# Padding the gate-decay matmuls to 128 rows and splitting the second FFN product by its high and low parts

## The chip, the cores and the metric

The kernel runs on one core of a Trainium2 chip. The metric is the device time of one execution in microseconds (us). The engines are named as in the profile: PE (matrix products; PEld is its weight loads), DVE (vector), ACT (scalar), POOL (GpSimd) and SP (queue that issues most DMAs). SBUF is the on-chip memory, PSUM holds the products of PE.

## What is computed

An mLSTM layer with exponential gates, over 4 batches, 8 heads, 768 steps and heads of width 40, followed by a gated feed-forward layer (FFN) of width 1024:

```python
m_new = np.maximum(f_gate[:, :, t] + m, i_gate[:, :, t])
f_stab = np.exp(f_gate[:, :, t] + m - m_new)
i_stab = np.exp(i_gate[:, :, t] - m_new)
C = f_stab[..., None, None] * C + i_stab[..., None, None] * np.einsum('bhd,bhe->bhde', vt, kt)
n = f_stab[..., None] * n + i_stab[..., None] * kt
h_tilde = np.einsum('bhde,bhe->bhd', C, qt)
denom = np.maximum(np.abs(np.einsum('bhd,bhd->bh', n, qt)), 1.0)[..., None]
y[:, :, t] = sigmoid(o_gate[:, :, t]) * h_tilde / denom
...
h = np.maximum(x @ w_in, 0.0)                    # x: the heads side by side, width 320
conv_out[:, t] = sum(conv_w[k] * h[:, t + k - 1] for k in range(3))
out = (h * sigmoid(conv_out)) @ w_out
```

## The kernel before

**Tiling.** The 768 steps of a batch are cut into 6 chunks of 128, so there are 24 chunks s; two chunks make one of 12 units u of 256 steps for the FFN. Within a chunk attention is a matrix product with decays; between chunks a state `Cst` (40 x 41 per head, three heads side by side in a group, so 120 rows) carries over.

**Gates.** `gates` (L242 to L258) runs two scans and two sums over 32 rows (batch x head) on DVE for a group of chunks. `GS` cuts the 6 chunks into groups (0,1), (1,2), (2,6), so the last group is four chunks wide. `gates_t` transposes the results on PE and `gates_tc` copies them out: `aT` on DVE (L306), `wT` on ACT (L308).

**Decays.** For the first three chunks (`NP` = 3) the decays are spread by PE: `ch_gpe` (L401) adds a triangular mask (one matmul of 512 columns, L405) and then, per head, a product of one column of the identity, repeated 128 times, with the 32 rows of `Gt` (L408). For all later chunks a DMA spreads them from DRAM and POOL masks them (L432). ACT takes the exponential (`ch_exp`, L439).

**Attention of a chunk.** `ch_s` (L464) forms scores in PSUM, `ch_p` (L471, DVE) multiplies by the decays, `ch_inter` (L482) multiplies the queries with the masked state `cb`, `ch_pv` (L491) adds the products with the values into the same PSUM tile `pY`, of which there is one. `ch_rden` makes the denominator, `ch_num` (L547, DVE) divides out of `pY` into `x`, `ch_x` (L554, DVE) applies the output gate on `x` in SBUF, `ch_t` (L575) transposes it, `ch_split` and `ch_splitl` (L213, L589, L590) cut it into a high and a low part. `ch_u` and `ch_state` (L502, L515) advance the state, `ch_cb` (L518) multiplies it with a mask of 120 x 369 numbers, `mk_sb`: two instructions, all on POOL.

**Weights.** `w_in` and `w_out` come as 64-bit numbers, 17 loads with the convolution's weights; each is converted by one ACT, four DVE (or POOL) instructions (`w_abs` L326, `w_max` L330, `w_conv` L339, L341, L343) and cut into a high and a low part.

**FFN of a unit.** Eight blocks f of 128 columns. `f_m1` (L618) is eight matmuls; `f_relu`, `f_tap1`, `f_tap` (L628, L636, L650) make the convolution, then for each pair of blocks `f_tanh`, `f_g` (L654, L658), `f_gh` (the high part, ACT, L213) and `f_gl` (the low part, POOL, L209). `f_m2` (L672) multiplies for each block f and each half k of the unit three times (L681): high part by high weights, high part by low weights, low part by high weights, into two PSUM tiles `po`. `f_out` (L683) evicts both halves on one engine and `f_outd` stores them.

**Order.** Every step is a job with costs by engine, a priority (`z` plus an offset by kind, `OFF`), an earliest time (`REL`, `SLOPE`) and the jobs that it follows. `order` (L85) is a list scheduler that runs when the program is built: it fixes the order in which each engine gets its instructions; on the chip each engine runs its own list in that order and waits by semaphores. It also puts in products of zeros (`warm`, L358, one call is two instructions) where it plans a gap of PE, after 16 such calls at the start.

Of the kernel before, what the change touches and what calls it, by code (L numbers as in the profile page):

```python
# [28 lines left out]
GS = ((0, 1), (1, 2), (2, 6))  # L29
OFF = dict(  # L30
    gpe=-466.23, loadw=661.3, mask=-269.35, loadn=-68.02, o=280.76, exp=294.49, wk=-126.2, u=148.37, state=-639.08,
    cb=374.33, s0=-143.64, s1=77.22, p0=75.42, p1=778.82, inter=-156.65, pv0=139.58, pv1=72.13, rd0=-530.16,
    rd1=-177.78, rd2=-366.75, num=-71.97, x=-364.12, dup=-443.23, t=134.98, split=-103.1, splitl=-629.56, halo=-96.74,
    xnew=770.29, kz=422.26, eg=-465.52, qe=-64.53, m1=68.78, relu=280.55, tap1=-76.28, tap0=-31.97, tap2=-344.77,
    tanh=-878.29, g=-168.6, gh=-221.34, gl=-54.96, m2=172.63, out=-699.14, outd=-271.95, wld=-396.31, wabs=113.45,
    wc0=142.39, wc1=134.61, wc2=-231.53, wc3=-361.52, wsh=-403.2, wsl=-141.82, g0=139.41, ga0=-702.7, gw0=202.06,
    ge0=-294.32, gd0=185.74, gg0=-506.27, ta0=-379.4, tc0=84.31, tw0=-397.4, tx0=499.3, g1=-646.44, ga1=106.16,
    gw1=-15.09, ge1=-15.86, gd1=135.02, gg1=240.52, ta1=81.59, tc1=-75.67, tw1=-9.9, tx1=-551.62, g2=489.66,
    ga2=-137.32, gw2=-158.94, ge2=92.62, gd2=-67.67, gg2=-504.91, ta2=-274.22, tc2=-450.62, tw2=-181.8, tx2=-88.05,
# [27 lines left out]
FREE0 = dict(PE=6.15, DVE=3.5, ACT=5.8, POOL=5.2, SP=1.6)
# [18 lines left out]
def order(jobs, pre):  # L86
# [31 lines left out]
    while len(done) < len(jobs):  # L118
# [42 lines left out]
        else:  # L161
            d = j["cost"][e]
            if e == "PE":
# [10 lines left out]
                for a, b, w in spans:  # L174
                    while a < b:
# [3 lines left out]
                        if c <= a:  # L179
                            break  # L180
# [693 lines left out]
```

## Time and profile before

| what | value |
|---|---|
| median of 3 runs | 345.4 us (345.09 to 349.81) |
| the profiled execution | 344.72 us |
| its span, first to last instruction | 342.6 us |
| mean granted clock of PE | 0.959 |
| PE, DVE, ACT, POOL busy | 328.7, 262.9, 236.3, 202.7 us |

Times in the rows below are from the span's start. A "busy" PE is one with a matmul in flight, which at the lower of its two clock levels says little about work done, so the granted clock of a stretch is read beside it. The idle time that stands in a row is that of the engine just before the instruction, with the engine and the tile that ended it.

### The profile page before, as it was taken

How to read it: one execution, taken by the hardware profiler on the slowest of the kernel's cores; microseconds unless marked ns; L12 is line 12 of the kernel's file. 1: busy time of each engine (PE TensorE's matmuls, PEld its weight loads, DVE VectorE, ACT ScalarE, POOL GpSimd, SP SyncE). 2: the span in 40 equal slices, each digit the busy share in tenths (PEclk: the TensorE clock that was granted, in tenths of full speed). 3: DMA queues.
4: the chain of work that ended last, by engine and by line, in shares of the span. 5: the costliest groups of instructions: out<-in, count | busy, mean ns of one | idle time of the engine just before them, and what ended most of it. 6: DMA issues, size and time to landing. Idle time of an engine off the chain costs nothing.

```text
span 342.6 us, 7422 instructions
## 1 busy us (share of the span) xinstructions
PE 328.7 (96%) x2534; PEld 322.3 (94%) x2534; DVE 262.9 (77%) x598; ACT 236.3 (69%) x610; POOL 202.7 (59%) x310
## 2 busy tenths in 40 slices
PE   7699898998999999999999999999999999999995
PEld 7588898999999999999999999999999999999995
DVE  4897889999998987778489877676888768566750
ACT  2355747879988668896958786769685536577871
POOL 7369898869968647584745661746563234343341
PEclk9855599999999999999999999999999999999999
DMA  6887658686717466174315452654211001010111
GB/s 167 273 250 299 215 196 271 192 256 180 221 53 219 150 194 205 64 216 157 101 58 153 127 160 93 187 182 147 94 59 41 0 2 38 2 38 2 38 41 38
DMA packets 18575, 46.09 MB, mean 135 GB/s; under 512 B 2579, under 2 KB 6347, under 8 KB 18539
## 3 DMA queue, kind: packets, MB, share of 16 engines
q1 hardware_dynamic: 18068, 45.22, 42.4%
q8 instruction: 20, 0.33, 0.5%
q10 hardware_dynamic: 471, 0.41, 0.4%
q14 instruction: 16, 0.13, 0.1%
HBM read 41.49 MB, written 4.13 MB: 133 GB/s over the span
## 4 chain that ended last, share of the span: by engine, by line
PE 71%; DVE 11%; POOL 6%; ACT 4%; DMA 3%; issue 3%; SPq 0%; POOLq 0%; DVEq 0%; ACTq 0%
PE po L681 22%; PE ph L618 22%; PE pY L491 10%; PE pS L464 9%; PE pY L482 3%; PE pU L502 3%; PE pT L575 2%; DMA wraw<-in_w_in 1%; DVE cv L650 1%; DVE ph L650 1%; ACT w L439 1%; DMA w<-G_d 1%; PE pg L408 1%; POOL gl L209 1%; POOL w L432 1%
## 5 line engine op out<-in xcount | busy, mean ns | idle before, releaser
L209 POOL TENSOR_TENSOR gl<-cv,gh 128x512 fp32r<-128x512 f32 x48 | 62.5, 1302 | 47.4 <-ACT gh L213 40.7
L618 PE MATMUL ph<-X,wi_h 128*128 128x258 f32 x480 | 77.1, 290 | 2.2 <-DVE cv L650 1.5
L618 PEld LDWEIGHTS ph<-X,wi_h 128*128 128x128 f32 x480 | 64.6, 190 | 3.0 <-ACT ph L636 1.7
L681 PE MATMUL po<-wo_h,gh 128*128 128x320 f32 x192 | 61.5, 320 | 0.5 <-ACT ot L687 0.5
L439 ACT ACTIVATE w<-w,aT 128x128 f32<-128x128 f32 x168 | 55.1, 391 | 8.1 <-POOL w L432 8.1
L650 DVE SCALAR_TENSOR_TENSOR ph<-h,cw_sb,ph 128x256 f32<-128x256 f32 x96 | 46.1, 483 | 18.9 <-ACT ph L636 18.4
L681 PE MATMUL po<-wo_l,gh 128*128 128x320 f32 x192 | 59.3, 309 | 0.0
L681 PE MATMUL po<-wo_h,gl 128*128 128x320 f32 x192 | 59.3, 309 | 0.0
L464 PE MATMUL pS<-q,kz 120*128 120x128 f32 (+1 forms) x384 | 53.1, 287 | 4.2 <-DVE aT L306 3.1
L464 PEld LDWEIGHTS pS<-q,kz 120*128 120x128 f32 (+1 forms) x384 | 48.6, 199 | 4.6 <-DVE aT L306 3.2
L658 DVE SCALAR_TENSOR_TENSOR cv<-cv,h 128x512 f32<-128x512 f32 x48 | 40.4, 844 | 15.9 <-ACT cv L654 15.6
L628 ACT ACTIVATE h<-ph 128x258 f32<-128x258 f32 x96 | 36.5, 380 | 23.1 <-PE ph L618 21.2
L650 DVE SCALAR_TENSOR_TENSOR cv<-h,cw_sb,ph 128x256 f32<-128x256 f32 x96 | 45.1, 476 | 8.1 <-POOL gl L209 4.9
L618 PE MATMUL ph<-X,wi_l 128*128 128x258 f32 x288 | 50.3, 283 | 0.0
L491 PE MATMUL pY<-n,w 128*128 128x41 f32 x384 | 47.8, 282 | 0.0
L491 PEld LDWEIGHTS pY<-n,w 128*128 128x128 f32 x384 | 47.2, 197 | 0.2
L636 ACT ACTIVATE ph<-h,cw_sb 128x256 f32<-128x256 f32 x96 | 45.6, 475 | 1.9
L654 ACT ACTIVATE cv<-cv 128x512 f32<-128x512 f32 x48 | 30.1, 627 | 16.3 <-DVE cv L650 9.3
L618 PEld LDWEIGHTS ph<-X,wi_l 128*128 128x128 f32 x288 | 41.3, 190 | 0.0
L213 ACT ACTIVATE gh<-cv 128x512 fp32r<-128x512 f32 x48 | 30.0, 624 | 11.2 <-PE po L681 11.2
L681 PEld LDWEIGHTS po<-wo_h,gh 128*128 128x128 f32 x192 | 36.2, 188 | 0.7 <-ACT ot L687 0.7
L681 PEld LDWEIGHTS po<-wo_l,gh 128*128 128x128 f32 x192 | 36.2, 189 | 0.0
(84 smaller groups left out, 530.0 us busy)
## 6 DMA issues: line engine op xcount, KB each, us to landing
n<-in_nat SPq DMA_DIRECT2D x24, 484.0 KB
w<-G_d SPq DMA_DIRECT2D x21, 512.0 KB
q<-in_qT SPq DMA_DIRECT2D x12, 360.0 KB
out<-ot SPq DMA_DIRECT2D x24, 160.0 KB
wraw<-in_w_in SPq DMA_DIRECT2D x8, 384.0 KB
kz<-in_kT SPq DMA_DIRECT2D x24, 120.0 KB
eq<-E_d SPq DMA_DIRECT2D x24, 120.0 KB
wraw<-in_w_out SPq DMA_DIRECT2D x8, 320.0 KB
```

What stands on the lines that cost most here:

```text
L209: (nc.gpsimd if e == "POOL" else nc.vector).tensor_tensor(out=out, in0=in0, in1=in1, op=op)
L213: nc.scalar.activation(out, in_, AF.Copy)
L439: nc.scalar.activation(w[:, h, :], g, AF.Exp, bias=aT[:, c, b * 8 + h : b * 8 + h + 1])
L464: nc.tensor.matmul(pS[:, j, :], lhsT=lhsT, rhs=rhs, start=(j == 0), stop=(j == 3), skip_group_check=True)
L491: nc.tensor.matmul(pY[:, h * VW : (h + 1) * VW], lhsT=r["w"][:, n, :], rhs=v[:, DM + h * VW : DM + (h + 1) * VW], start=(c == 0 and n == 0 ...
L618: nc.tensor.matmul(ph, lhsT=a, rhs=b_, start=(i == 0), stop=(i == len(mm) - 1))
L628: nc.scalar.activation(hj, ph, AF.Relu)
L636: nc.scalar.activation(c, hk, AF.Copy, scale=wk)
L650: nc.vector.scalar_tensor_tensor(o, hk, wk, c, op0=ALU.mult, op1=ALU.add)
L654: nc.scalar.activation(cv, cv, AF.Tanh, scale=0.5)
L658: nc.vector.scalar_tensor_tensor(cv, cv, 1.0, h[:, :, 1 : 1 + UT], op0=ALU.add, op1=ALU.mult)
L681: nc.tensor.matmul(obuf[u][k], lhsT=a, rhs=b_, start=(f == 0 and i == 0), stop=(f == 7 and i == 2))
```

## The change

1. `Gt` becomes the first 32 rows of a tile `Gz` of 128 rows; the other 96 rows are set to zero by two DVE instructions. The spread of the decays multiplies all 128 rows.
2. `GS` has four groups: (0,1), (1,2), (2,4), (4,6).
3. The mask is 120 x 3 numbers, and `ch_cb` is three ACT instructions with a scale per row, in place of two POOL ones. POOL clears `Cst` once at the start.
4. `ch_num` divides in place in PSUM; `ch_x` reads PSUM and writes `x`. So `pY` is held until `x` is done, and not only until `num` is.
5. `m2` becomes two jobs for each block: `m2` (high part, two matmuls for each half) that waits for `gh`, and `m2l` (low part, one for each half) that waits for `gl` and `m2`. `gl` must now be done before `gh`'s buffer is used again.
6. `out` and `outd` become one job for each half.
7. The starting calls of `warm` go from 16 to 9, the planner's constants and offsets are new, and a table `FIX` gives the jobs of the first six chunks, of all weights, of the first two units and of the end priorities and earliest times of their own.

```diff
-GS = ((0, 1), (1, 2), (2, 6))
+GS = ((0, 1), (1, 2), (2, 4), (4, 6))
...
-    Gt = const.tile([32, S], F32, name="Gt")
+    Gz = const.tile([P, S], F32, name="Gz")
+    nc.vector.memset(Gz[32:64, :], 0.0)
+    nc.vector.memset(Gz[64:P, :], 0.0)
+    Gt = Gz[0:32, :]
...
-            nc.tensor.matmul(p[:, j, :], lhsT=id_sb[0:32, r : r + 1].to_broadcast([32, P]), rhs=Gt[:, c * P : (c + 1) * P],
+            nc.tensor.matmul(p[:, j, :], lhsT=id_sb[:, r : r + 1].to_broadcast([P, P]), rhs=Gz[:, c * P : (c + 1) * P],
...
+    nc.gpsimd.memset(Cst, 0.0)
...
-    def ch_cb(e, s):
+    def ch_cb(s):
         cb = sb.tile([120, 3, 123], F32, name="cb", tag="cb")
-        mk3 = mk_sb.rearrange("p (g v) -> p g v", g=3)
-        tt(e, cb[:, 0:2, :], Cst[:, 0:2, :], mk3[:, 0:2, :], ALU.mult)
-        tt(e, cb[0:80, 2, 0:82], Cst[0:80, 2, 0:82], mk3[0:80, 2, 0:82], ALU.mult)
+        for j in range(3):
+            ng, sl = 3 if j < 2 else 2, slice(j * VW, (j + 1) * VW)
+            nc.scalar.activation(cb[:, 0:ng, sl], Cst[:, 0:ng, sl], AF.Copy, scale=mk_sb[:, j : j + 1])
...
     def ch_num(s):
...
-        nc.vector.tensor_tensor(x, y3[:, :, 0:D], r["rd"].unsqueeze(2).to_broadcast([P, H, D]), op=ALU.mult)
-        r["x"] = xf
+        nc.vector.tensor_tensor(y3, y3, r["rd"].unsqueeze(2).to_broadcast([P, H, D]), op=ALU.mult)
 
     def ch_x(s):
...
-        nc.vector.scalar_tensor_tensor(xf[:, 0:DM], o, 1.0, xf[:, 0:DM], op0=ALU.add, op1=ALU.mult)
+        nc.vector.scalar_tensor_tensor(x, o, 1.0, y3, op0=ALU.add, op1=ALU.mult)
...
-    def f_m2(u, f):
+    def f_m2(u, f, low):
...
+        ws = [wo_h[:, f, :]] if low else [wo_h[:, f, :], wo_l[:, f, :]]
         for k in range(2):
-            mm = ((gh[:, j, ks], wo_h[:, f, :]), (gh[:, j, ks], wo_l[:, f, :]), (gl[:, j, ks], wo_h[:, f, :]))
+            for i, w in enumerate(ws):
+                nc.tensor.matmul(obuf[u][k], lhsT=g[:, j, k * P : (k + 1) * P], rhs=w, start=(f == 0 and not low and i == 0), stop=(f == 7 and low == 1))
...
-        at("inter", z, qe + [("cb", us - 1)] if c else [], ch_inter, s, ring="y", users=[("num", s), ("rd1", s)], cost=0.63 if c else 0.01)
+        at("inter", z, qe + [("cb", us - 1)] if c else [], ch_inter, s, ring="y", users=[("x", s)], cost=0.63 if c else 0.01)
...
-            at("m2", n, [("gl", 4 * u + f // 2), ("wsl", 8 + f)] + ...
+            at("m2", n, [("gh", 4 * u + f // 2), ("wsl", 8 + f)] + ...
+            at("m2l", n, [("gl", 4 * u + f // 2), ("m2", n)] + ([("m2l", n - 1)] if n else []), f_m2, u, f, 1)
+        for k in range(2):
+            at(f"out{k}", 8 * u, [("m2", 8 * u + 7), ("m2l", 8 * u + 7)], f_out, u, k, ring="ot", users=[(f"outd{k}", u)])
+            at(f"outd{k}", 8 * u, [(f"out{k}", u)], f_outd, u, k)
```

## Rows read from the trace of the kernel before

**Rows 1.** Busy time and granted clock by stretch: us, busy us of each engine (instructions), PEclk, DMA.

```profile
14.10:41.40 27.30, 24.79 (x103) 21.60 (x104) 24.30 (x46) 17.14 (x53) 21.23 (x34) 0.50 0.78 263
41.40:60.00 18.60, 17.09 (x150) 16.57 (x150) 16.27 (x41) 11.09 (x34) 17.45 (x28) 1.00 0.74 233
60.00:140.00 80.00, 78.11 (x651) 77.10 (x650) 73.13 (x178) 65.75 (x186) 59.72 (x94) 1.00 0.60 179
140.00:300.00 160.00, 160.00 (x1300) 159.92 (x1299) 118.94 (x276) 111.87 (x274) 82.20 (x132) 1.00 0.32 101
```

**Rows 2.** PE in order of time, front: start, length in us, work, idle before.

```profile
1.81 6.45 PE L358 MATMUL pw<-wz 128*128 128x128 f32 x32 [1.81 <-POOL wz L352]
8.02 0.48 PE L405 MATMUL pg<-tri 128*128 128x512 f32 x1
...
15.52 2.08 PE L464 MATMUL pS<-q,kz 120*128 120x128 f32 x8 [3.07 <-DVE aT L306]
...
20.98 2.07 PE L408 MATMUL pg<-Gt,id_sb 32*128 32x128 f32 x8
...
23.89 3.64 PE L491 MATMUL pY<-n,w 128*128 128x41 f32 x16
...
37.63 2.05 PE L464 MATMUL pS<-q,kz 120*128 120x128 f32 x8 [1.09 <-DVE X L590]
...
41.81 1.99 PE L464 MATMUL pS<-q,kz 120*128 120x128 f32 x16
```

**Rows 3.** ACT in order of time, the start, as in rows 2.

```profile
6.74 0.31 ACT L228 ACTIVATE tri<-ltm 128x128 fp32r<-128x128 f32 x1 [2.34 <-DMA ltm<-in_tr]
```

**Rows 4.** Waits in the first 50 us: us in total, times, longest us.

```profile
DVE rd L534 <- PE pY L491: 2.3, 1, 2.3
...
DVE w L471 <- PE pS L464: 1.4, 2, 1.2
```

**Rows 5.** DVE in order of time, 9 to 16 us, as in rows 2.

```profile
10.22 0.36 DVE L330 TENSOR_SCALAR wmag<-wmag 128x384 f32<-128x384 f32 x1 [1.40 <-ACT wmag L326]
10.49 1.27 DVE L246 TENSOR_TENSOR_SCAN mt<-ft,mt,it 32x512 f32<-32x512 f32 x1
...
12.51 1.63 DVE L254 TENSOR_TENSOR Gt<-Gt,mt 32x512 f32<-32x512 f32 x1
...
15.31 0.15 DVE L306 COPY aT<-pt 128x32 f32<-128x32 f32 x1
15.55 2.15 DVE L330 TENSOR_SCALAR wmag<-wmag 128x384 f32<-128x384 f32 x1
```

**Rows 6.** Groups by line: instructions, busy us, mean ns of one, idle before.

```profile
L209 POOL TENSOR_TENSOR cb<-Cst,mk_sb 120x246 f32<-120x246 f32 (+1 forms) x40 | 22.3, 577 | 5.5 <-DVE Cst L513 5.0 <-DVE Cst L515 0.5
...
L554 DVE SCALAR_TENSOR_TENSOR x<-n,x 128x320 f32<-128x320 f32 x24 | 14.7, 612 | 0.3
...
L343 DVE SCALAR_TENSOR_TENSOR wf<-wraw,wf 128x384 int32<-128x384 int32 (+1 forms) x16 | 12.5, 787 | 0.1
...
L547 DVE TENSOR_TENSOR x<-pY,rd 128x320 f32<-128x320 f32 x24 | 11.7, 486 | 0.5
...
L213 ACT ACTIVATE x<-x 128x64 f32<-128x64 f32 x15 | 3.7, 250 | 5.9 <-DVE x L554 5.9
```

**Rows 7.** The instructions of L554: least, median and most ns, first and last start.

```profile
L554 DVE SCALAR_TENSOR_TENSOR x<-n,x x24: 479/491/1429, 30.3 to 295.1; 128x320 f32<-128x320 f32 x24
```

**Rows 8.** PE waits from 60 us on, as in rows 3.

```profile
PE ph L618 <- DVE cv L650: 1.5, 3, 0.9
PE ph L618 <- ACT wo_h L213: 0.6, 1, 0.6
PE po L681 <- ACT ot L687: 0.5, 1, 0.5
```

**Rows 9.** The end in order of time, as in rows 2.

```profile
338.52 0.88 ACT L687 ACTIVATE ot<-po 128x320 f32<-128x320 f32 x2 [4.36 <-PE po L681]
...
338.98 0.81 SPq L697 DMA_DIRECT2D out<-ot  x2
```

More of the change, by code (lines that the diff above doesn't have):

```diff
@@ L28 @@
 NP = 3
-GS = ((0, 1), (1, 2), (2, 6))
+GS = ((0, 1), (1, 2), (2, 4), (4, 6))
 OFF = dict(
[L31 to L39, printed above, removed]
+    gpe=-344.57, loadw=386.08, mask=-26.16, loadn=-394.15, o=-181.8, exp=70.24, wk=770.38, u=192.04, state=-1136.15,
+    cb=67.88, s0=-26.21, s1=-70.13, p0=-46.84, p1=613.63, inter=-64.06, pv0=-149.84, pv1=183.19, rd0=-458.38,
+    rd1=317.06, rd2=44.69, num=240.44, x=-176.22, dup=-280.33, t=0.34, split=-477.58, splitl=-551.94, halo=707.01,
+    xnew=519.63, kz=587.22, eg=-855.33, qe=-350.16, m1=-325.28, relu=1032.41, tap1=524.79, tap0=425.34, tap2=-683.42,
+    tanh=-1075.16, g=671.8, gh=-291.83, gl=-383.62, m2=201.38, m2l=-101.96, out0=-623.0, out1=-1227.56, outd0=326.25,
+    outd1=-827.38, wld=-245.4, wabs=-503.59, wc0=409.0, wc1=-103.8, wc2=-242.53, wc3=-156.55, wsh=-57.39, wsl=22.55,
+    g0=309.26, ga0=-1001.88, gw0=567.53, ge0=-30.73, gd0=422.34, gg0=-115.72, ta0=-925.37, tc0=497.34, tw0=-909.0,
+    tx0=86.89, g1=-869.76, ga1=-9.02, gw1=-285.94, ge1=442.53, gd1=-323.21, gg1=825.83, ta1=251.86, tc1=-874.62,
+    tw1=-724.52, tx1=-888.57, g2=526.67, ga2=131.53, gw2=395.8, ge2=-152.56, gd2=28.74, gg2=-1624.6, ta2=-994.23,
+    tc2=135.74, tw2=-1117.02, tx2=-359.37, g3=406.55, ga3=-332.79, gw3=-594.14, ge3=98.49, gd3=-458.1, gg3=-1097.12,
+    ta3=-419.62, tc3=-408.2, tw3=-812.34, tx3=-372.69,
 )
@@ L67 @@
[L67 removed]
+    g2={"DVE": 2.4}, ga2={"POOL": 2.0, "DVE": 0.8}, gw2={"POOL": 0.8, "DVE": 0.4}, ge2={"ACT": 0.4}, gd2={"SP": (0.45, 0.8)}, gg2={"SP": (0.45, 0.8)},
+    ta2={"PE": 0.3}, tc2={"DVE": 0.1}, tw2={"PE": 0.3}, tx2={"ACT": 0.25},
+    g3={"DVE": 2.4}, ga3={"POOL": 2.0, "DVE": 0.8}, gw3={"POOL": 0.8, "DVE": 0.4}, ge3={"ACT": 0.4}, gd3={"SP": (0.45, 0.8)}, gg3={"SP": (0.45, 0.8)},
+    ta3={"PE": 0.3}, tc3={"DVE": 0.1}, tw3={"PE": 0.3}, tx3={"ACT": 0.25},
+)
@@ L73 @@
 LAG, PELAG = 0.035, 0.3
-SWAP = {'DVE': 2.13, 'POOL': -0.08, 'ACT': 0.51}
+SWAP = {'DVE': 31.6, 'POOL': 17.07, 'ACT': -8.31}
 DMALAG = (0.65, 0.7)
-ACT_W = dict(pv0=0.3, pv1=0.3, gpe=0.4)
-HAM = (3.4133, 0.37, 0.92)
-WARM = (6.0, 60.0, 16)
+ACT_W = dict(pv0=0.3, pv1=0.3, s=0.5, ta0=0.3, ta1=0.3, ta2=0.3, ta3=0.3, tw0=0.3, tw1=0.3, tw2=0.3, tw3=0.3)
+HAM = (3.4133, 0.4, 0.92, 0.5)
+WARM = (5.0, 60.0, 9, 1.8, 0.22)
 def holds(key, eng):
@@ L94, in order, with busy @@
     ready = {}
-    win, act = [0, False], {0: 1.5, 1: 2.73}
+    win, act = [0, False], {}
+    def busy(a, b, w):
+        while a < b:
+            k = int((a - HAM[3]) / HAM[0] + 1e-9)
+            c = min(b, HAM[3] + (k + 1) * HAM[0])
+            act[k] = act.get(k, 0.0) + (c - a) * w
+            if c <= a:
+                break
+            a = c
+    busy(WARM[3], FREE0["PE"], 1.0)
     queue = {e: [] for e in free}
@@ L847 @@
     w_in = np.stack([wi[0:128], wi[128:256], np.concatenate([wi[256:320], wi[256:320]])], axis=2)
-    msk = np.zeros((3, D, 3, 3, VW), np.float32)
-    for j in range(3):
-        msk[j, :, :, j, :] = 1.0
+    msk = np.repeat(np.eye(3, dtype=np.float32), D, axis=0)
     arrays = {
```

213 lines of the change are left out of this document (148 added, 65 removed).

## The prediction, made before the change was run

> **What bounds the kernel now.** I read the busy times by stretch first. From 140 to 300 us PE is busy 160.00 of 160.00 us at the full clock, while DVE has 118.94 and ACT 111.87: there PE sets the pace, and the change leaves PE's number of products as it is. From 60 to 140 us PE still has 78.11 of 80.00, with DVE at 73.13 [rows 1]. So whatever a change can gain must come from before 60 us, from the few waits after it, or from the end.
>
> [...]
>
> The order of PE shows what came before and after the low level. Before it fell PE idled 3.07 us, up to 15.52, for DVE's copy of `aT`. In the low stretch it ran spreads of 32 rows (20.98 us) and products with values 41 columns wide (23.89 us); before it rose it ran, from 37.63 us on, scores, state and inter products without a spread [rows 2]. DVE's order shows why `aT` was late: the copy at 15.31 stood behind the gates of four chunks, from 10.49 on, and these behind a weight instruction that had waited 1.40 us for its load [rows 5].
>
> The sum is made against the profiled execution, 344.72 us, of which 342.6 are its span and 2.1 lie around it; the median of the runs is 345.4, 0.7 more, so I take the sum's gain from 345.4.
>
> **The change part by part.**
>
> *Spread over 128 rows.* The number and width of the products stay (48 plus 6), and the score products, with 120 rows, run at the pace of the 32-row ones (eight in 2.08 against 2.07 us [rows 2]), so rows cost PE nothing. What it can give is the clock. If it gives nothing: 0. If the whole stretch ran at the upper level and only PE mattered: half of 24.79, 12.4 us. But DVE's 24.30 us of work stay in the stretch, which then can shrink by 27.30 - 24.30 = 3.0 us, and just behind it DVE waits again for slow products: DVE's waits for `pY` and for scores that a slow PE ended are 2.3 and 1.4 us [rows 1, 4]. I take their sum, 3.7, as nearest to how the two engines stand, and keep 0 and 12.4. [...]
>
> The clearing of the 96 rows is two DVE instructions; the nearest row is an instruction on 128x384 numbers, 0.36 us [rows 5], so 768 columns twice are 1.4 us. They need no input, while DVE's first gate waits for two loads, so I take 0; without that cover they delay the first gate by 1.4.
>
> *Four groups of gates.* The four-chunk chain took 15.31 - 10.49 = 4.8 us; two halves put the copies of `aT` up to 2.4 us earlier. DVE does the same sums and some five instructions more, at the 0.15 us of the small copy [rows 5] 0.75 us; two more DMAs for `G_d` and `E_d` go on SP, and PE gets no more transposes. From -2.4 to +0.75; since DVE, and not the wait, fills what follows, I take -1.0.
>
> *`cb` to ACT.* POOL loses 22.3 us, ACT gains 60 instructions. The nearest row is the 128x64 copy, 0.250 us [rows 6], so 15 us or a little more, 0.75 for each of 20 chunks. From 60 to 140 us ACT has 65.75 of 80 [rows 1]; some 6 chunks there add 4.5, which leaves 9.7 idle. That slack covers it; without it each `cb` would put 0.75 before its inter products. What POOL gives back: its work stretches some DVE instructions, 2.15 us against 0.36 for the same form [rows 5]; the weight instruction L343 has a mean of 0.787 [rows 6]. For 384 columns the median of `x`, 0.491 us for 320 columns [rows 7], would make 0.59, so L343 is stretched by 16 x 0.20 = 3.2 us, and the four conversion lines together by an estimated 12.8. About a tenth of POOL's work goes, and with it a tenth of that, 1.3. From 0 to 1.3, I take 1.0.
>
> *`num` in place, `x` from PSUM.* `x`, which reads SBUF twice, has a median of 0.491 us but a most of 1.429, mean 0.612 [rows 6, 7]; `num`, which reads PSUM, has a mean of 0.486 [rows 6]. If reading PSUM spares `x` the stretching, 24 x (0.612 - 0.486) = 3.0 us of DVE, half of it, 1.5, in the part where DVE is full. Against it `pY` stays taken 0.49 longer: `inter`, `pv0` and `pv1` of the next chunk queue behind that on PE, and DVE's next denominator behind them. In the dense front, chunks 2 to 5, this costs 0 to 4 x 0.49 = 2.0; I take 0.5, one such wait. Net -1.0, between -1.5 and +2.0. [...]
>
> *`m2` and `m2l`.* The same matmuls. The high part no longer waits for `gl`, so PE has work to put where it now waits for DVE and ACT: 1.5 and 0.6 us after 60 us [rows 8]. From 0 to -2.1; I take -1.0. What is late next is the same convolution, on DVE.
>
> *Output halves.* Both halves still wait for the last `m2l`, and the stores follow 0.46 us behind the first eviction [rows 9] as before, with SP taking 0.81 for two. The 0.5 us for which a unit's first product waits on the evictions [rows 8] stays too. 0; at best the second eviction's 0.44, half of 0.88 [rows 9], is saved.
>
> *Smaller edits.* Sixteen starting calls held PE from 1.81 for 6.45 us, to 8.26, about when the first spread ran, 8.02 [rows 2]; the mask in `tri` was ready at 6.74 + 0.31 = 7.05 [rows 3]. Seven calls less could bring the spread 1.0 us forward, but the scores' exponentials waited for `aT` at 15.31 [rows 5], so 0. The smaller mask saves a transfer in the first 10 us, when weights are late by 1.40 [rows 5]; 0 to 1.4, I take 0.3. The new order as such I cannot price: 0, and 6 us either way in the range.
>
> Sum: 3.7 + 1.0 + 1.0 + 1.0 + 1.0 + 0.3 = 8.0, and 345.4 - 8.0 = 337.4 us.
>
> **The rivals.**
>
> *Forecast: the clock stays or comes back early, and DVE sets the front's pace.* 333 to 341 us. For it: DVE's 24.30 of 27.30 and 73.13 of 80. Chance 0.48.
>
> *PE sets the front's pace.* With the weights' conversions put behind attention, DVE can be made to wait less and all 12.4 us come back: 337.4 - (12.4 - 3.7) = 328.7. For it: a single wrong place (gates behind a late weight) opened the 3.07 us idle; against it: DVE is still full up to 140 us, and what is put off must be done there. Chance 0.22.
>
> *The clock's gain does not come.* The rows of the spread are not what held the clock down, or the list opens a new idle time of PE like that before 15.52. Then the sum without 3.7 is 341.1, and with the doubtful 1.0s of `cb` and `m2` gone as well 343.1. For it: products 41 columns wide fill the low stretch too and stay as they are. [...] Chance 0.20.
>
> *Slower: the planned zero products run into a low clock.* The list puts products of zeros wherever it plans PE idle in the front. If it plans the upper level and gets the lower, real work of 12.4 us plus up to 14.9 of zeros in those 27.3 us takes twice as long. Each zero microsecond planned then holds back the attention queued behind it by one more. With the clock's 3.7 gone the other terms are 4.3, so above 4.3 us of zeros the sum turns to a loss; at 14.9 it is 345.4 + 14.9 - 4.3 = 356.0. For it: the list is fixed when the program is built and cannot see the clock; against it: the zeros are themselves dense work on 128 rows. Chance 0.10.
>
> **How the numbers follow.** A difference under 2%, 6.9 us, is about what a measurement can't tell from no change: faster means below 338.5, slower above 352.3. The forecast's 333 to 341 lies to two thirds below 338.5: 0.32 faster, 0.16 same. The large gain adds 0.22 faster, the lost clock 0.20 same, the slow case 0.07 slower and 0.03 same. Faster 0.54, same 0.39, slower 0.07. The range goes from 327 to 346, which leaves out the slow case and the far end of the large gain.
>
> **What would show it.** Right: PEclk of 1.00 in most of 14 to 41 us; no idle time of some 3 us of PE before 15 us; L554's most near 0.5; the first FFN product before 59 us; no `gl` on POOL among what PE waits for. Wrong: a low stretch of 27 us again, or many more L358 instructions than 44 with a front no shorter; PE waits for `x` before `pY`; ACT above 76 of 80 us from 60 to 140, with PE waiting for `gh`.

## The result, and the profile after

The changed kernel takes 348.55 us (median of 19 runs, 344.6 to 351.63) beside 345.09 us for the kernel before on the same chip (19 runs, 344.21 to 349.81). The ratio, taken over the executions within 1.5% of each kernel's fastest, is 1.0078, 95% interval 1.0059 to 1.0097: 0.8% slower. The median is 11 us above the forecast of 337.4 and outside its range. The profiled execution has a span of 346.8 us, 4.2 more than that of before.

Busy times by stretch, kernel after (us; busy us of each engine and its instructions; granted clock, DMA share, GB/s):

```profile
14.10:41.40 27.30, 23.37 (x194) 21.91 (x192) 22.91 (x55) 14.92 (x46) 19.69 (x32) 1.00 0.90 279
41.40:60.00 18.60, 17.22 (x152) 16.96 (x152) 16.98 (x41) 14.46 (x47) 12.79 (x23) 1.00 0.85 273
60.00:140.00 80.00, 74.56 (x602) 72.65 (x602) 70.11 (x165) 70.16 (x208) 49.76 (x82) 0.98 0.59 181
140.00:300.00 160.00, 158.59 (x1267) 157.29 (x1267) 112.12 (x258) 120.29 (x312) 70.08 (x99) 1.00 0.30 94
```

Against [rows 1]: the front has its clock back, 1.00 in place of 0.50. But from 60 to 140 us PE falls from 78.11 to 74.56 of 80, and the clock to 0.98. ACT's busy time there goes up from 65.75 to 70.16 and POOL's down by 10 us.

What PE waited for in the whole span, kernel after (total us, times, longest), some of the lines:

```profile
PE ph L727 <- DVE cv L759: 3.0, 4, 1.5
PE pS L574 <- DVE aT L416: 2.4, 1, 2.4
...
PE pT L684 <- ACT x L320: 1.2, 1, 1.2
PE pY L592 <- ACT wo_h L320: 1.0, 1, 1.0
...
PE po L789 <- POOL wo_l L316: 0.7, 1, 0.7
...
PE pY L592 <- DVE x L663: 0.3, 1, 0.3
```

Several of them fall close together. PE in order of time, kernel after (start, length, work, idle before):

```profile
92.65 0.87 PE L592 MATMUL pY<-cb,eq 120*128 120x123 f32 x6 [0.87 <-issue]
...
99.17 0.41 PE L789 MATMUL po<-wo_l,gh 128*128 128x320 f32 x1 [0.66 <-POOL wo_l L316]
...
100.95 0.87 PE L727 MATMUL ph<-X,wi_h 128*128 128x258 f32 x5 [1.07 <-DVE cv L759]
...
110.16 0.87 PE L592 MATMUL pY<-cb,eq 120*128 120x123 f32 x6 [1.02 <-ACT wo_h L320]
110.86 2.13 PE L601 MATMUL pY<-n,w 128*128 128x41 f32 x16
112.79 1.42 PE L727 MATMUL ph<-X,wi_h 128*128 128x258 f32 x5
...
249.35 0.33 PE L684 MATMUL pT<-id_sb,x 128*128 128x128 f32 x1 [1.18 <-ACT x L320]
```

The engine that a wait is put down to is inferred, so I set it against the times of what the product needs. DVE, ACT and POOL in order of time, kernel after, as above:

```profile
92.07 0.48 DVE L663 SCALAR_TENSOR_TENSOR x<-n,pY 128x320 f32<-128x320 f32 x1
...
97.93 2.06 DVE L649 TENSOR_SCALAR rd<-rd 128x8 f32<-128x8 f32 x1
...
98.27 1.69 POOL L316 TENSOR_TENSOR wo_l<-wf,wo_h 128x320 fp32r<-128x320 f32 x2
...
100.41 0.48 DVE L759 SCALAR_TENSOR_TENSOR cv<-h,cw_sb,ph 128x256 f32<-128x256 f32 x1
...
104.32 0.94 ACT L633 ACTIVATE cb<-Cst,mk_sb 120x123 f32<-120x123 f32 x3
...
109.57 0.48 DVE L663 SCALAR_TENSOR_TENSOR x<-n,pY 128x320 f32<-128x320 f32 x1
```

The inter product at 110.16 is put down to ACT's `wo_h`, but the `cb` that it reads was done at 105.26. What ended just before it is `x` of the chunk before, at 110.05, which holds the one `pY` (item 4 of the change); the product at 92.65 likewise follows an `x` that ended at 92.55. Counted in this way, the first product of a chunk came 0.10 to 0.32 us behind the end of the last chunk's `x` after an idle PE six times in the kernel after: 3.9 us in all, at 41.85, 50.19, 58.08, 77.05, 92.65 and 110.16. At most 3.4 of them lie between the end of `num` and the end of `x`. In before, where `num` frees `pY`, it happens once, for 0.52 us. The wait for `cv` at 100.95 follows a DVE instruction on 128x8 numbers that took 2.06 us, where the median of its ten is 0.228; it ended at 99.99, and POOL's pair of `wo_l` at 99.96.

From 112.4 to 115.8 us the granted clock is at the lower level, 0.50: five products at 112.79 take 1.42 us where five at 100.95 take 0.87.

Busy shares hide what this costs, so I count PE's useful work: each of the kernel's own matmuls, zeros left out, at the time between two starts of its kind at the full clock (0.105 to 0.147 us by the traces; the kernel's sum is 302.9 us in every trace). Done by a given time, in us:

| by | 41.4 | 60 | 90 | 120 | 140 | 240 | 260 | last product ends |
|---|---|---|---|---|---|---|---|---|
| before | 13.5 | 28.6 | 57.2 | 86.1 | 105.5 | 205.6 | 225.5 | 338.9 |
| after | 18.1 | 32.4 | 59.9 | 83.8 | 103.4 | 203.0 | 220.8 | 343.1 |

After leads by 3.8 us at 60 and by 2.7 at 90; at 120 it is 2.3 behind, so 5.0 us are lost in 30. Another 2.1 go between 240 and 260, around the wait at 249.35. ACT, which that wait is put down to, had itself stood idle 2.44 us up to 246.99 for the load of `n`.

The loss from 90 to 120 can be added up from the rows. PE is idle there for 3.62 us, where before has 0.70: 1.89 for `pY`, 1.07 for `cv`, 0.66 for `wo_l`. The 3.4 us at a granted clock of 0.50 cost an estimated 1.7, half of them. Together that is 2.9 and 1.7, or 4.6 of the 5.0 us. The table is the case: the gain came, and was given back where the prediction took PE to be full.

### The profile page after: what moved, and what is told of

Its sections match the earlier page's. It is cut to its first block, busy times and chain, and to the rows that moved or that the text cites. A ratio compares the mean times of both kernels' runs of the same rounds, so it can differ in the third digit from the quotient of the medians.

```text
span 346.8 us, 7580 instructions
## 1 busy us (share of the span) xinstructions
PE 327.9 (95%) x2606; PEld 321.6 (93%) x2606; DVE 259.2 (75%) x600; ACT 252.1 (73%) x690; POOL 173.6 (50%) x261
## 4 chain that ended last, share of the span: by engine, by line
PE 69%; DMA 10%; DVE 9%; ACT 9%; issue 2%; SPq 1%; ACTq 0%; POOL 0%; DVEq 0%
PE po L789 23%; PE ph L727 23%; PE pS L574 8%; PE pY L601 7%; DMA n<-in_nat 5%; ACT w L549 3%; PE pY L592 3%; PE pU L613 2%; DMA wraw<-in_w_in 2%; DMA ltm<-in_tr 1%; PE pT L684 1%; DVE w L581 1%; DMA w<-G_d 1%; PE pw L468 1%; DMA wraw<-in_w_out 1%
## 5 line engine op out<-in xcount | busy, mean ns | idle before, releaser
L316 POOL TENSOR_TENSOR gl<-cv,gh 128x512 fp32r<-128x512 f32 x48 | 62.4, 1303 | 85.2 <-ACT gh L320 76.1
L727 PE MATMUL ph<-X,wi_h 128*128 128x258 f32 x480 | 78.0, 293 | 3.2 <-DVE cv L759 3.0
L727 PEld LDWEIGHTS ph<-X,wi_h 128*128 128x128 f32 x480 | 65.3, 191 | 4.8 <-DVE cv L759 2.3
L759 DVE SCALAR_TENSOR_TENSOR ph<-h,cw_sb,ph 128x256 f32<-128x256 f32 x96 | 46.5, 485 | 18.1 <-ACT ph L745 16.3
L789 PE MATMUL po<-wo_h,gh 128*128 128x320 f32 x192 | 59.6, 319 | 0.0
L789 PE MATMUL po<-wo_l,gh 128*128 128x320 f32 x192 | 58.2, 311 | 0.7 <-POOL wo_l L316 0.7
L549 ACT ACTIVATE w<-w,aT 128x128 f32<-128x128 f32 x168 | 56.3, 391 | 2.7 <-POOL w L542 2.7
L574 PE MATMUL pS<-q,kz 120*128 120x128 f32 (+1 forms) x384 | 50.2, 277 | 3.2 <-DVE aT L416 2.4
L767 DVE SCALAR_TENSOR_TENSOR cv<-cv,h 128x512 f32<-128x512 f32 x48 | 37.0, 773 | 18.3 <-ACT cv L763 18.2
L574 PEld LDWEIGHTS pS<-q,kz 120*128 120x128 f32 (+1 forms) x384 | 46.1, 191 | 3.6 <-DVE aT L416 2.5
L601 PEld LDWEIGHTS pY<-n,w 128*128 128x128 f32 x384 | 46.4, 192 | 1.2 <-DVE w L581 0.5
L737 ACT ACTIVATE h<-ph 128x258 f32<-128x258 f32 x96 | 36.3, 378 | 13.9 <-PE ph L727 12.7
L789 PE MATMUL po<-wo_h,gl 128*128 128x320 f32 x192 | 42.3, 311 | 0.0
L763 ACT ACTIVATE cv<-cv 128x512 f32<-128x512 f32 x48 | 30.1, 628 | 14.7 <-DVE cv L759 14.5
L320 ACT ACTIVATE gh<-cv 128x512 fp32r<-128x512 f32 x48 | 30.1, 626 | 7.4 <-PE po L789 5.4
```

The lines of the kernel that those rows point to most:

```text
L316: (nc.gpsimd if e == "POOL" else nc.vector).tensor_tensor(out=out, in0=in0, in1=in1, op=op)
L320: nc.scalar.activation(out, in_, AF.Copy)
L549: nc.scalar.activation(w[:, h, :], g, AF.Exp, bias=aT[:, c, b * 8 + h : b * 8 + h + 1])
L574: nc.tensor.matmul(pS[:, j, :], lhsT=lhsT, rhs=rhs, start=(j == 0), stop=(j == 3), skip_group_check=True)
L601: nc.tensor.matmul(pY[:, h * VW : (h + 1) * VW], lhsT=r["w"][:, n, :], rhs=v[:, DM + h * VW : DM + (h + 1) * VW], start=(c == 0 and n == 0 ...
L727: nc.tensor.matmul(ph, lhsT=a, rhs=b_, start=(i == 0), stop=(i == len(mm) - 1))
```

## The experiments

Except where said, "before" in a ratio is the kernel before, run beside it on the same chip. A median is of all executions.

**1. The control.** The changed kernel again.

> The changed kernel once more, on the chip of these runs, as their control: 346 to 351 us.

348.64 us, ratio 1.0099 (1.007 to 1.0128). Its useful work is 30.6 by 60, 82.8 by 120 and 220.2 by 260 us: the same shape, though the lead over before at 60 us is 2.0 and not 3.8. This execution has a low stretch in the front, from 31.9 to 35.3 us, and the waits at 94.34, 101.99 and 111.19 us that the other has at 92.65, 100.95 and 110.16.

**2. The clock and the 128 rows.** Before with only the spread over 128 rows (e1); after with 32 rows (e2); before with 128 rows and 14 calls of zeros in the 3 us of idle time ahead of the second half of the first chunk's scores (e8).

```diff
 e1, on before; e2 is the reverse, on after
-lhsT=id_sb[0:32, r : r + 1].to_broadcast([32, P]), rhs=Gt[:, c * P : (c + 1) * P]
+lhsT=id_sb[:, r : r + 1].to_broadcast([P, P]), rhs=Gz[:, c * P : (c + 1) * P]
 e8, in addition to e1
+        if e in (("s0", 0), ("s1", 0)):
+            done_s.append(e)
+            if len(done_s) == 2:
+                warm(14)
```

> The kernel before with one edit: the spread of the decays multiplies 128 rows, 96 of them zero; list and all else as before. Theory A (the clock in the front is held down by what PE runs there, the 32-row spreads among it, and the profile after shows it up): the low stretch of 27.3 us gets shorter by at least half, and the time falls by 2 to 5 us, to 340 to 343 us, because DVE then sets the pace. Rival B (the 3 us idle time of PE before 15.5 us brings the clock down and the spread has no say): the same 27 us at the lower level, 345 us. Rival C (the clock comes back but nothing in the front is bound by PE): low stretch short, time within 1 us of 345.

> The changed kernel with only the spread put back to 32 rows; list and all else as changed. Theory A (rows decide): a low stretch of 10 us or more appears between 10 and 45 us and the time rises from 348.5 by 2 to 6 us. Rival B (the zero products and the new order keep the clock up): granted clock 0.99 as in the changed kernel, 348 to 349 us.

> The kernel before with the spread over 128 rows and 14 calls of the product of zeros (28 instructions) put where PE waited 3 us for the copy of the gates, before the second half of the first chunk's scores. This asks what the clock of the front is worth by itself. Theory K (the low stretch costs some 3.7 us, since DVE waits for slow products there): low stretch gone, 340 to 342 us, first FFN product 3 us or more before 59.9 us. Rival L (with DVE nearly full a faster PE only waits more): low stretch gone, first FFN product 3 us earlier or less, 344 to 346 us, and more idle time of PE behind 60 us. Rival M (the idle time is not what brings the clock down): low stretch as before.

e1: 347.63 us, ratio 1.001 (0.9985 to 1.0036), mean clock of the executions counted 0.965 to 0.979 where before has 0.955 to 0.965, so some of the low stretch may have gone in some of them, and the time did not follow. Its profiled execution is the odd one of the last section, so its trace is not read for this. e5 below has the 128 rows under the old planner, and its trace is at the lower level, 0.50, for 27.3 us in all, as before's is. e2: four runs, 346.78, 346.89, 353.17 and 354.24 us, mean clock 0.994 in its profile, with one low stretch from 30.1 to 33.5 us; the control has one of the same length. So the rows did not bring the clock back in the old list and are not what keeps it up in the new one; something in the new list does. It has 116 instructions on zeros up to 49.6 us where before has 44, and they are the likely reason, but they were not taken out alone. e8: 345.66 us, ratio 1.0025 (0.9998 to 1.0052). Its stretches, and two rows of PE:

```profile
14.10:41.40 27.30, 16.75 (x109) 15.26 (x108) 24.16 (x46) 17.54 (x54) 21.97 (x34) 0.78 0.81 264
41.40:60.00 18.60, 18.60 (x118) 18.49 (x118) 11.41 (x28) 7.09 (x22) 13.55 (x25) 0.68 0.52 156
...
26.56 0.79 PE L408 MATMUL pg<-tri 128*128 128x512 f32 x1 [4.11 <-ACT w L442]
...
37.15 2.04 PE L467 MATMUL pS<-q,kz 120*128 120x128 f32 x8 [4.41 <-DVE X L593]
```

Up to 41.4 us the clock rose to 0.78, PE's busy time fell from 24.79 to 16.75 us, and the useful work is 13.8 where before has 13.5. DVE still has 24.16 of 27.30 us: at a better clock PE only waited longer there, for ACT and DVE. But the low stretch was moved more than removed. The clock fell in these two waits, and was at the lower level from 22.6 to 29.4 and from 36.3 to 53.3 us, 23.9 us in all where before has 27.3. By 60 us the useful work is 25.9 where before has 28.6, and the first FFN product comes at 64.1 and not at 59.9. So a front of the old list at the upper level all through, as theory K has it, was not reached, and what it would be worth is not known.

**3. One edit alone on before.** `cb` on ACT (e13); `x` from PSUM (e14); the second product as two jobs, the outputs as halves (e16, with 128 rows; its list is made anew by the planner of before).

```diff
 e13
-        tt(e, cb[:, 0:2, :], Cst[:, 0:2, :], mk3[:, 0:2, :], ALU.mult)
-        tt(e, cb[0:80, 2, 0:82], Cst[0:80, 2, 0:82], mk3[0:80, 2, 0:82], ALU.mult)
+            nc.scalar.activation(cb[:, 0:ng, sl], Cst[:, 0:ng, sl], AF.Copy, scale=mk_sb[:, j : j + 1])
 e14
-        nc.vector.tensor_tensor(x, y3[:, :, 0:D], r["rd"].unsqueeze(2).to_broadcast([P, H, D]), op=ALU.mult)
+        nc.vector.tensor_tensor(y3, y3, r["rd"].unsqueeze(2).to_broadcast([P, H, D]), op=ALU.mult)
 e16
-    m2={"PE": 0.88}, out={"ACT": 0.64, "DVE": 0.8}
+    m2={"PE": 0.585}, m2l={"PE": 0.295}, out0={"ACT": 0.34, "DVE": 0.4}, out1={"ACT": 0.34, "DVE": 0.4}
```

> The kernel before with cb made by three copies of ACT with a scale in place of two products on POOL, in the same place of the list. [...] Rival (ACT's queue has cb behind exp and o, which the list was not made for): cb comes late, PE waits for ACT before pY, and the time is 346 to 349 us.

> The kernel before with num left in PSUM and x read from there, nothing else. [...] Rival (x from PSUM waits as much for POOL, or the bank held longer delays the next pY): no change, 345 to 346.5 us.

> The kernel before, with its planner and its costs, but the second FFN product as two jobs of the list and the output as two halves; cb on POOL and x through SBUF as before; the decays spread over 128 rows, which alone measured 1.001. By the prediction's term the two jobs give back 1.0 us: 344 to 345 us. Rival (before's planner makes a worse list from the finer jobs; with all edits under it the time was 350.1 us): 348 to 351 us, and then neither cb nor x made that run slow.

By the prediction's terms, 1.0 us each, e13 and e14 come to 344 us. e13: 346.07 us, ratio 1.0056 (1.0023 to 1.009). e14: 362.12 us, ratio 1.0474 (1.0404 to 1.0545). e16: 352.36 us, ratio 1.0232 (1.0205 to 1.026). None gives a microsecond back. What PE waited for in e14 (some of the lines):

```profile
PE pY L482 <- DVE x L552: 5.2, 5, 2.0
PE pS L464 <- DVE aT L306: 3.6, 1, 3.6
PE pY L482 <- POOL w L432: 2.6, 1, 2.6
```

Before's list lets `x` come long after `num`. With `pY` held until `x`, PE stood for it. By the ends of `x`, as above, it did so eleven times, up to 2.6 us, 11.4 us in all; the wait put down to POOL's `w` is one of them. The chain then slid further than these waits: the useful work by 120 us is 71.9, 14.2 less than before, and the mean clock is 0.941 where before has 0.959.

**4. All edits under the old planner, and single edits undone under the new list.** e5 has the new code with before's planner, costs and three gate groups; e3 puts `cb` back on POOL, e4 `x` back through SBUF, both in the changed kernel; e10 there moves the high parts of `w_out` and the copies of `x` from ACT to POOL.

```diff
 e3, on after
-            nc.scalar.activation(cb[:, 0:ng, sl], Cst[:, 0:ng, sl], AF.Copy, scale=mk_sb[:, j : j + 1])
+        tt("POOL", cb[:, 0:2, :], Cst[:, 0:2, :], mk3[:, 0:2, :], ALU.mult)
+        tt("POOL", cb[0:80, 2, 0:82], Cst[0:80, 2, 0:82], mk3[0:80, 2, 0:82], ALU.mult)
 e4, on after
-        nc.vector.scalar_tensor_tensor(x, o, 1.0, y3, op0=ALU.add, op1=ALU.mult)
+        nc.vector.scalar_tensor_tensor(xf[:, 0:DM], o, 1.0, xf[:, 0:DM], op0=ALU.add, op1=ALU.mult)
 e5, on after
-GS = ((0, 1), (1, 2), (2, 4), (4, 6))
+GS = ((0, 1), (1, 2), (2, 6))
+FIX = {}
 e10, on after
+        if e[0] == "dup" or (e[0] == "wsh" and e[1] >= 8):
+            j["eng"] = "POOL"
```

> All code edits of the change (128 rows, masked state on ACT, division in PSUM, FFN product in two jobs, output halves, small mask), but the planner of the kernel before: its three groups of gates, priorities, offsets and release times, no table; the new jobs take the offsets of the old ones. Theory H (the new list costs what the code edits and the clock win): 339 to 343 us, below the kernel before, PE busy 99% from 60 to 140 us. Rival I (the code edits themselves cost, the longer hold of the PSUM tile and the load on ACT): 347 us or more with PE waits for the masked state or for the tile between 60 and 140 us. Rival J (nothing but the front's clock matters): about 345.

> The changed kernel with the masked state made on POOL again, by two instructions and the mask of 120 x 369 numbers, at the same place of the list. In the changed kernel ACT is busy 9.3 to 9.6 of 10 us between 70 and 100 us, and PE loses there what it gained before 60 us. Theory D (ACT is what holds PE back there, and the 0.85 us of each masked state on it are the cause): PE's waits between 60 and 110 us fall by half, the time falls by 2 to 4 us, to 344.5 to 346.5. Rival E (the order of the list is at fault, whichever engine makes the masked state): within 1 us of 348.5, or 0.3 us later for each chunk of the front, 349 to 350, since POOL takes 1.1 us for it.

> The changed kernel with the division written to SBUF and the gate applied there again, so the PSUM tile of the next chunk's inter product is free half a microsecond earlier. Theory F (the longer hold of that tile costs): the time falls by 1 to 3 us. Rival G (DVE's stretched instructions on SBUF come back): L-lines of x show a most above 1 us again, and the time rises by 0.5 to 1.5 us. Theory E (the order): within 0.7 us of 348.5.

> The changed kernel with ACT relieved where it is nearly full: the high parts of w_out (8 instructions of 0.47 us) and the copies of 64 columns of x (24 of 0.25 us) go to POOL, at the same places of the list. POOL is idle half the time there. Theory D (ACT as the engine that is full between 70 and 110 us holds PE back): PE's waits in 60 to 110 us, 5.3 us of idle time in the profile after, fall by half and the time falls by 2 to 4 us, to 345 or 346. Rival E (the order and the latency of each link, not the load of ACT): within 1 us of 348.5, with the waits moved to other links.

e5: 350.07 us, ratio 1.0157 (1.0115 to 1.0199). e3: 357.08 us, 1.036 (1.0317 to 1.0402). e4: four runs from 348.89 to 369.11 us; the fastest is level with the changed kernel and the others are 9 us or more above it, so no verdict follows. In its profile (359.29 us) PE's waits for `pY` are down to 0.35 us, `x` from SBUF takes up to 1.443 us again, and the clock is at the lower level for 20 us in four pieces. e10: 351.91 us, 1.0218 (1.0162 to 1.0273). So e3, e5, e10, e14 and e16, each an edit made or undone under a list that was not made for it, cost more than the whole change does; e1 and e13 cost less. Such runs price the edit together with its misfit; they can't price the edit. In e10 ACT's load fell (246.4 us busy in all where after has 252.1), and PE waited, by the ends of `x`, 4.7 us for `x` before `pY`, and 1.9 us for `wo_l`: the load of ACT alone is not the cause.

**5. The late conversions.** In after the third and fourth low part of `w_out` start at 98.3 and 99.1 us, in before at 78.1 and 87.3, and the idle time at 99.17 waits for one of them. So entries of the new list, these conversions, two `gh` and `gl` and second products of unit 0, were moved ahead by hand (50 in the kernel's table, where the expectation says 46).

```diff
-    for e in order(jobs, pre):
+    at_t, t = [], 0.0
+    for e in order(jobs, pre):
+        t = order.t.get(e, t)
+        at_t.append((moved.get(e, t), len(at_t), e))
+    for _, _, e in sorted(at_t):
```

> The changed kernel with 46 entries of its list moved ahead and nothing else changed: the conversions of the w_out pieces 11 to 16, whose low parts came done at 98 to 125 us where the kernel before had them at 78 to 123, gh and gl of the second and third pair of unit 0 with what they need, and the second FFN products 2 to 5 of unit 0. Theory W (the late conversions and gh leave TensorE without second FFN products from 90 to 120 us, where 5.0 us of its work were lost against before): the useful work by 120 us comes back to 85 or 86 us from 83, TensorE's idle stretches at 91.6, 98.1 and 108.9 go, the low clock of 112.4 to 115.8 with them, and the time is 343 to 346 us. Rival (the stretch from 90 to 120 is short of ACT, DVE and POOL together, and whatever is moved ahead pushes attention back): work by 120 stays at 82 to 84 us, new waits of PE for DVE appear, 347.5 to 351 us.

356.06 us, ratio 1.0314 (1.028 to 1.0348), and 79.9 us of useful work by 120. From the third on the low parts came 9 to 23 us sooner, and PE waited for `x` before `pY` for 7.1 us in all, by the ends of `x`, up to 1.8 at a time. That theory fell in the form in which it could be tried: an entry moved ahead stands in its engine's list before whatever it passes, and these waits for `x` went from the 3.9 us of the changed kernel to 7.1.

**6. The same jobs in another order.** The planner may place each job anew if its due times change; the code is the same. With the places come the planner's zeros (42 instructions in e5, 96 in e18, 92 in e20, 118 in e17) and, for a few jobs, another engine. e18 and e20 have the code of e5 with two sets of due times found apart; e17 is the changed kernel with another set.

```diff
+DUE = dict(...)   # some 1,300 to 1,800 due times
...
+        z1, rel = DUE.get(key, {}).get(n, (z1, rel))
         jobs[key, n] = dict(cost=COST[key] if cost is None else {eng: cost}, z=z1, rel=rel, ...
```

> All code edits of the change (decays over 128 rows, cb on ACT, x from PSUM, the second FFN product as two jobs, output halves; three gate groups) as in the run with the planner of before, which took 350.1 us, but with other due times for its jobs, so that the same instructions come in another order: the first FFN product some 10 us sooner, w_out's third to sixth low part at 74 to 96 us and not at 98 to 110, second FFN products in a steady row from 64 us on. Theory O (the edits are worth what the prediction says or more, and only the list lost it): 335 to 343 us, useful work by 60 us of 32 or more and by 120 us of 86 or more. Rival (the edits cost more than they give, in ACT's load and in pY's bank, under any list): 346 us or more, with PE waiting for ACT or for x before pY again.

> The same code with a third set of due times, found apart from the other. Theory O: again below 345 us, within some 4 us of the other new list. Rival (a list made from costs says little of the chip, and an order suits or not by chance): the two lists come out more than 6 us apart, or both above 345 us.

> The changed kernel with its own planner and other due times for the same jobs, w_out's low parts from the third on at 91 to 121 us in the list and not 98 to 125, so no more than a small change of the order. Theory O: 344 to 347 us, useful work by 120 us a little above 84. Rival (the changed kernel's list is fitted to what the chip does in a way that due times made from costs miss, as in the run with w_out moved ahead by hand): 350 us or more.

e18: 345.27 us, ratio 0.9996 (0.9964 to 1.0027). e20: 348.08 us, 1.0114 (1.0071 to 1.0156). e17: 347.94 us, 1.0084 (1.007 to 1.0098). The order, with the zeros that come with it, is worth 4.8 us between e5 and e18. But theory O's 335 to 343 us did not come either. Useful work by time:

| by | 41.4 | 60 | 90 | 100 | 120 | 140 | 260 | last product ends |
|---|---|---|---|---|---|---|---|---|
| before | 13.5 | 28.6 | 57.2 | 67.2 | 86.1 | 105.5 | 225.5 | 338.9 |
| e5 | 14.1 | 27.2 | 53.1 | 62.4 | 82.2 | 101.5 | 221.1 | 343.7 |
| e18 | 22.6 | 35.6 | 61.7 | 69.3 | 87.3 | 107.3 | 226.9 | 337.6 |
| e20 | 21.4 | 35.7 | 56.6 | 66.3 | 85.8 | 103.3 | 223.8 | 342.1 |

e18 leads before by 7.0 us at 60, by 1.2 at 120. The execution in the table is its fastest, 343.02 us, 2.25 under its median. e20 leads by 7.1 at 60 and is 0.3 behind at 120; most of that goes between 60 and 90 us, where PE stands idle 4.95 us up to 68.16, right behind the end of an `x` at 68.01, and the granted clock is 0.89. So it is not the changed kernel's list alone: in three lists most or all of a lead at 60 us is gone by 120. But the loss of a lead is not the whole of it either: e17, the changed kernel in a slightly other order, has 27.8 us of useful work by 60, 0.8 behind before, 83.4 by 120 and 221.0 by 260, and takes as long as the changed kernel. The stretch in e18:

```profile
60.00:140.00 80.00, 74.85 (x611) 72.87 (x611) 71.67 (x175) 66.75 (x190) 57.88 (x88) 0.99 0.64 192
```

and what PE waited for there (window 60 to 140 us):

```profile
PE ph L709 <- DVE cv L741: 1.7, 2, 1.5
PE pY L574 <- DVE x L645: 1.5, 1, 1.5
PE po L771 <- POOL wo_l L298: 1.3, 2, 0.7
```

**7. Is it DVE?** DVE has 70 to 73 of 80 us in that stretch in before, after and e18 and heads these waits. So the same 16 DVE instructions, the second and third step of `w_out`'s conversion, were left out of after, before and e18, with the lists unchanged. The output is then that of other weights, and each conversion's own chain is shorter too, so load and chain are not told apart.

```diff
     def w_conv(key, n, dst, k):
+        if k > 1 and key[0] == "o":
+            return
```

> The changed kernel with its list as it is; left out are the second and third step of the conversion of w_out's eight pieces, 16 instructions of DVE of 0.48 us or more, some 8 to 9 us of DVE's work between 54 and 124 us (so the output is that of other weights). Theory D (from 60 to 120 us DVE, with ACT next to it, sets the pace, so that a gain of TensorE's in the front is given back there): useful work of TensorE by 120 us rises from 83.8 to 87 us or more, its waits for cv shrink, and the time falls by 3 us or more to 345 us or less. Rival (the order on TensorE's own queue, or the chain of chunks, sets the pace there and DVE does not): 347 to 349 us.

> The same 16 instructions of DVE left out of the kernel before (again other weights in the output). By theory D TensorE is already full from 60 to 140 us there but for 2 us of waits, since it comes to that stretch 3.8 us later and DVE keeps up: no more than 1 to 2.5 us, 342.5 to 344 us. Rival: if DVE's total work up to 120 us is what counts in either kernel, both fall by the same.

> The same 16 instructions left out of the code with the other list, whose TensorE stands 7.0 us ahead of before at 60 us and only 1.2 ahead at 120. By theory D this is where most comes back: useful work by 120 us 90 or more (87.3 with them), 338 to 342 us. Rival: no more than 1 us, 344 to 346 us.

After: 348.44 us, ratio 1.0106 (1.0055 to 1.0157), no gain clear of noise. Before: 343.74, 0.9971 (0.9959 to 0.9984), 1.3 us less. e18's list: 342.78, 0.9915 (0.9874 to 0.9956), 2.5 us less than e18. The stretch of 60 to 140 us of the three, in this order:

```profile
60.00:140.00 80.00, 75.61 (x624) 73.91 (x624) 64.21 (x154) 71.98 (x215) 50.30 (x86) 1.00 0.57 181
```

```profile
60.00:140.00 80.00, 78.83 (x657) 77.91 (x657) 68.84 (x164) 66.06 (x188) 60.03 (x95) 1.00 0.58 183
```

```profile
60.00:140.00 80.00, 76.16 (x628) 74.49 (x629) 66.94 (x168) 68.90 (x196) 56.67 (x88) 1.00 0.67 201
```

DVE lost 5.9, 4.3 and 4.7 us of its work there, and PE came no nearer to 80 than 75.61 and 76.16 in the two new lists. DVE's load is a part of it in e18's list, as theory D said, though less than it said (88.3 us of useful work by 120, not 90). For the changed kernel theory D is not borne out: its median stays, though its profiled execution, the fastest of five, has 86.3 us by 120, where 87 or more were expected. Neither ACT relieved (e10) nor DVE relieved (e21) gave the time back there.

## Why the prediction was wrong

**Right: the front's clock comes back.** PEclk is 1.00 from 14 to 41 us, and the first FFN product comes at 54.7 us and not at 59.9. Right with it: `x` from PSUM takes 0.47 to 0.49 us every time, so the most of 1.429 [rows 7] is gone. The rows of `x` after:

```profile
L663 DVE SCALAR_TENSOR_TENSOR x<-n,pY x24: 474/484/487, 31.1 to 317.2; 128x320 f32<-128x320 f32 x24
```

**The size by luck, and the wrong cause.** PE's lead at 60 us is 3.8 us where this term of the sum had 3.7. But the lead holds all that the change does to the front, the control's is 2.0, and e17's is none. The term was booked on the 128 rows, and e1, e2 and e5 show that the rows do next to nothing (ratio 1.001 in e1; the same 27.3 us at the lower level in e5; a mean clock of 0.994 with 32 rows in e2 beside 0.995 in after); the new list holds the clock. The rival in which the rows are not what held the clock down was right about the rows. Its 341.1 us missed as well, since the clock did come back, with the list.

**Wrong: the step from "PE is full after 60 us" to "what is won before 60 stays won".** The prediction read 78.11 of 80.00 us from 60 to 140 [rows 1], looked for the gain before that stretch, in its few waits or at the end, and took it as kept. It named DVE as full up to 140 us only against a rival's larger gain. The reading held for the order that was measured. Where PE came to the stretch 3.8 us sooner it was busy 74.56 of 80, and 7.0 us sooner (e18) 74.85; in after the lead of 3.8 at 60 us was 2.3 behind at 120. That PE was full in before because it came late and found its inputs ready fits this, but was not shown by itself. The figure to put beside 78.11 was DVE's 73.13 of 80 [rows 1], and above all its first half, in the kernel before and after:

```profile
60.00:100.00 40.00, 39.11 (x335) 38.69 (x334) 38.92 (x98) 34.52 (x99) 31.68 (x47) 1.00 0.62 182
...
60.00:100.00 40.00, 36.53 (x310) 35.38 (x309) 37.09 (x91) 36.75 (x113) 26.29 (x46) 1.00 0.69 215
```

With DVE at 38.92 of 40 us (third busy time) there was little room to feed a PE that came sooner. It is not the whole cause: after has more idle DVE in this half, not less (37.09), and leaving out DVE's work gave it no time back (e21); in e18's list it gave 2.5 us (e23). What PE stood for in after from 90 to 120 us was results that came late one by one: `pY` held by `x`, `cv`, `wo_l`. The prediction used DVE's load to bound the front's gain and not to ask whether the gain could be kept.

**Wrong: the order priced at 0, with 6 us either way.** With the same code, e5 and e18 lie 4.8 us apart, more than any term of the sum; in the changed kernel the waits of 90 to 120 us, with the low clock behind them, go with a loss of 5.0 us, and 2.1 more are lost from 240 to 260, 1.18 of them idle up to 249.35. The range reached to 346, 8.6 above a centre that held 8.0 us of gains.

**Mis-sized: `pY` held until `x`.** The term was 0.5 us, one wait, at most 2.0, and in the front alone. By the ends of `x` PE stood for it six times and 3.9 us, of which at most 3.4 are the longer hold: 1.8 us before 60, near the bound, and 2.1 from 60 to 120, where the prediction looked for none. Against this the gain on DVE was of the size that was read: `num` and `x` together take 23.5 us in after where they take 26.4 in before [rows 6], 2.9 less. Under a list made for an early release e14 took 17 us more, misfit and low clock with it. With the hold undone in the new list (e4) the waits went and the time did not fall, so 3.9 us of waits are not 3.9 us of time to be had.

**Not seen: the 1.0 for `cb` and the 1.0 for `m2` and `m2l`.** `cb` alone gave nothing back in before (e13: 346.07 us, ratio 1.0056). ACT's part was sized well:

```profile
L633 ACT ACTIVATE cb<-Cst,mk_sb 120x123 f32<-120x123 f32 (+1 forms) x60 | 18.9, 381 | 4.8 <-DVE Cst L626 4.4 <-DVE Cst L624 0.3
```

It takes 18.9 us where 15 or a little more were estimated, and ACT stayed at 70.16 of 80, below the 76 named as a warning. The gain on the other side, a DVE less disturbed by POOL, did not become time. (What the trace of before shows of it: the six `x` of 0.675 us or more ran beside POOL's work for 0.72 or more of their time, though four others that did so for 0.59 or more took 0.486 to 0.557 us.) `m2` and `m2l` could not be priced apart from a new list (e16).

**The signs.** All that the prediction named for "right" came out while the time went the other way. Of those for "wrong" one came out, PE's waits for `x` before `pY`, and it was easy to miss, since the profile puts all but 0.3 us of them down to others. The signs looked at the front and at single engines; none asked whether PE was still at 78 of 80 us from 60 to 140. That was the premise, and it is what failed.

**What stays open.** The waits that add up to the loss from 90 to 120 us are read from the trace; no run took them out and won the time back. ACT relieved, DVE relieved, `pY` freed early and the late conversions moved ahead each left the time the same or worse, under a list not made for them. Why the clock fell at 112.4 us is not shown. No version with the whole computation beat the kernel before; e18 equals it.

## What to carry to other kernels

A full engine is full for the order that was measured; before a gain ahead of it is booked, ask which engine would stop it if it came sooner, and read that engine's busy time in that stretch. In a kernel whose queues are planned by hand, an edit and its list are one thing: tried apart, each can look worse than both together, so price the order as the first term of the change. Check the engine that a wait is put down to against the end times of all that the instruction needs. Count useful work by time and not busy time: it shows in one table where a gain comes and where it goes.

## What the runs showed of the hardware

The kernel before with 128 rows ran once at 903.91 us; its other nine runs took 343.55 to 349.69. The records of that execution hold no change of the clock, and its granted clock is given as 1.00, yet its first FFN products have a mean of 575 ns, while DVE, ACT and POOL are busy for 259.8, 240.6 and 195.1 us in all, about as in before:

```profile
L621 PE MATMUL ph<-X,wi_h 128*128 128x258 f32 x480 | 188.2, 575 | 0.0
```

The same group in the profiled execution of before:

```profile
L618 PE MATMUL ph<-X,wi_h 128*128 128x258 f32 x480 | 77.1, 290 | 2.2 <-DVE cv L650 1.5 <-ACT wo_h L213 0.6
```

So PE ran there at about half its pace in before, 575 against 290 ns, while the granted clock is given as 1.00; nothing here shows why. A small DVE instruction took as long as POOL worked: L649 on 128x8 numbers, 0.228 us in the median, took 2.06 us in after and ended at 99.99, 0.03 behind POOL's pair of `wo_l`; in the control it took 1.59 and ended at 101.03, 0.04 behind the same pair. That POOL held it up is inferred from these ends and was not tested. And an idle time does not decide by itself about the clock: in after PE idled 2.36 us up to 28.53 and stayed at the upper level, 1.00, in e2 it idled 2.79 us up to 29.14 and ran at the lower one, 0.50, from 30.1 to 33.5. With shorter idle times, of 0.66 to 1.07 us from 92 to 110 us, after fell to the lower level at 112.4. In e18 a lower mean clock mostly goes with a longer time: the five runs with a mean clock of 0.993 or more take 343.02 to 344.8 us, the two at 0.980 take 347.44 and 347.59, though one at 0.985 takes 343.88.
